# A router, attention and expert kernel: the first batch's softmax sums handed out earlier, its splits untied, one weight norm a half block later

## The chip, the core and the metric

The kernel runs on one core of a Trainium2 chip. The core has five engines with a queue of instructions each: PE (TensorE, the matrix multiplications, with its weight loads shown as PEld), DVE (VectorE), ACT (ScalarE), POOL (GpSimd) and SP (SyncE, which here issues most DMA transfers). A queue is worked off in the order in which it was written, so an instruction that waits holds up all that stands behind it on its engine. The metric is the device time of one execution in microseconds, the median of several runs.

## What is computed

The reference has three parts: an attention over 32 memory slots for 4 batches and 8 heads, a gated projection, and a mixture of experts in which each token goes to its two best of eight experts.

```python
a = np.exp(phi - np.max(phi, axis=2, keepdims=True))
a = a / (np.sum(a, axis=2, keepdims=True) + 1e-09)
k_m = np.einsum('bhsm,bhsd->bhmd', a, k)
v_m = np.einsum('bhsm,bhsd->bhmd', a, v)
scores = scale * np.matmul(q, k_m.transpose(0, 1, 3, 2))
attn = np.exp(scores - np.max(scores, axis=-1, keepdims=True))
attn = attn / (np.sum(attn, axis=-1, keepdims=True) + 1e-09)
attn_out = np.matmul(attn, v_m)
...
gate = 1.0 / (1.0 + np.exp(-(x @ w_gate)))
x = gate * (x @ w_val) @ w_out
...
noisy_logits = x @ w_gate2 + np.log1p(np.exp(x @ w_noise)) * noise
top2 = np.argpartition(-noisy_logits, 2, axis=1)[:, :2]
out[mask] += top2_w[mask, k, None] * (np.maximum(x[mask] @ w1[e], 0.0) @ w2[e])
```

There are 2304 tokens of width 512, a gated layer 1536 wide, and experts 1024 wide.

## The kernel before

Products keep nearly full precision by splitting each operand into a high and a low half of 16 bits and adding three matrix products. So every tensor that goes into a product is first split: ACT writes the high half, DVE the low one.

**The opening** does three things at once. The first is the attention of batch 0, a generator that is advanced one step at a time (`attention`): `scores` of a group makes the products on PE, then on DVE the maximum (L286) and the difference (L290) and on ACT the exponential (L291). `normalised` sums the exponentials (L297), takes the reciprocal (L300, L301) and multiplies on POOL (L302). `turned` transposes on PE (L310) and splits, the high half on ACT (L319) and the low one on DVE (L320). There are three groups; the third is the short rest of the rows. In batch 0 the sum is written into the PSUM tile of the group's own scores, so that tile is free only when L300 has read it.

The second is the preparation of the weights (`weights`, `rounded`). Each of 18 jobs (six units u of gate and value weights, 12 jobs, then six jobs of the output weights `wo`) comes in two halves of 512 KB. A half is loaded by SP (L359), its low words are scaled on ACT (L370), its high words taken apart on DVE (L374, L375), and both added on POOL (L376). The tiles that the loads land in form a ring: while the output weights are prepared it has four tiles, so the load of a half waits until POOL is done with the half four places earlier. Here the twelve halves of the output weights are called h0 to h11. ACT squares and sums each job (L399, L416). From the sums of a unit `finish` makes a power of two as its scale: `norm2` adds over the partitions on PE (L93), and DVE works out scale and inverse (L99 to L104). After the last half of `wo` all sums are joined (L421), and `wo` is split by ACT (L431) and DVE (L432).

The third is stage 1 (`stage1`, L483 on PE; L485 and L488 on ACT; L487 and L489 on DVE) of the tokens whose attention is ready. Its weights come from `fold`, which multiplies the values into a unit's weights (L257 on PE, the scale on POOL at L250, the split at L259 on ACT and L261 on DVE; for the first unit the low half is made at L1085).

**What sets the order.** `build` writes the opening out as a loop. As long as batch 0 has no tokens ready, one half of a weight is rounded (`half`), then the attention is advanced by a step. After that each call of `first` (one unit of stage 1 on 192 tokens) is followed by three steps of the weights. Between these a scheduler orders by priority, and `behind` ties an instruction after another on the same engine: here DVE's steps of the attention are tied behind the last rounding (`shifted`). Once the weights are done, SP issues 23 transfers of zeros to the output (L578) and five more (L580), then the loads for batches 2 and 3. Stage 2 (L500), the router, and the experts (L847, L861) follow.

Of the kernel before, what the change touches and what calls it, by code (L numbers as in the profile page):

```python
# [68 lines left out]
class Kern:  # L69
# [196 lines left out]
    def attention(self, b):  # L266
# [38 lines left out]
        def turned(u, ex):  # L305
            nt = 1 if u == 2 else SC
            at = ex.rearrange("p (t h) m -> p t (h m)", t=nt)
            pt = self.bank(b)
            for t in range(nt):
                self.mark = nc.tensor.transpose(pt[:, t, :], at[:, t, :], self.idf)  # L310
                if b == 1:
                    self.behind(self.mark, self.gated)
            if u == 2:
                src = pt[:, 0, :].rearrange("p (g s) -> p g s", g=2)
                oh, ol = (x[:, l, :, SC * P :] for l in range(2))
            else:
                src = pt.rearrange("p a b -> p (a b)")
                oh, ol = (x[:, l, u, : SC * P] for l in range(2))
            nc.scalar.activation(oh, src, AF.Copy, scale=2.0 ** A_BITS)  # L319
            d = nc.vector.scalar_tensor_tensor(ol, src, 2.0 ** A_BITS, oh, op0=ALU.mult, op1=ALU.subtract)  # L320
            if b < 2:
                self.behind(d, self.shifted)
        part, ex = {}, {}
        for i in range(3):
            part[i] = scores(i)
            if b == 0 and i < 2:
                yield
                continue
            for j in range(3) if b == 0 else (i - 1,) if b == 1 and i else (i,) if b > 1 else ():
                ex[j] = normalised(*part[j])  # L330
                if b == 0:
                    yield
            if b:
                yield
        if b == 1:
            ex[2] = normalised(*part[2])
        if b:
            yield
        for i in range(3):
            turned(i, ex[i])  # L340
            yield
# [36 lines left out]
    def weights(self):  # L378
# [24 lines left out]
        for n, (kind, u) in enumerate(self.wjobs):  # L403
            v = self.flat(self.W[n]) if kind != "wo" else self.flat(self.wob[u + 1]).bitcast(F32)
            for h in range(2):
                self.rounded(self.wts[2 * n + h], v[:, h * 512 : (h + 1) * 512].bitcast(I32))
                self.wload_next()
                yield
                if h == 0 and 4 <= n <= 12:
                    square(n - 1)  # L410
                if h == 0 and 2 <= n <= 12 and n % 2 == 0:
                    yield from finish(n // 2 - 1, WAIT_W)
            if kind == "wo":
                for x in [u - 1] * (u > 0) + [u] * (u == UN - 1):
# [830 lines left out]
```

## Time and profile before

| | us |
|---|---|
| median of 3 runs | 856.12 |
| the three runs | 858.1, 853.94, 856.12 |
| profiled execution, whole time | 852.53 |
| its span in the trace | 850.7 |
| outside the span | 1.83 |

PE is busy for 796.5 us of the span, 94%; DVE for 454.2, ACT for 440.6 and POOL for 232.3. The span falls into a head of some 145 us, in which all engines share the work, and a long rest in which PE is hardly ever idle. In the trace, times count from the start of the span, a matmul's row has `PE`, its weight load `PEld`, and the square brackets at a row's end give how long the engine had been idle and what ended that. The clock column is the share of TensorE's full clock that was granted: 1.00 is 2.4 GHz and 0.50 is 1.2 GHz.

### The profile page before, as it was taken

The page shows a single profiled execution, that of the slowest core. Times are in us where ns is not written, and L with a number is a line of the kernel's source. Part 1 is how long each engine was busy: PE and PEld are TensorE (multiplying, and loading weights), DVE is VectorE, ACT ScalarE, POOL GpSimd, SP SyncE. Part 2 cuts the span into 40 slices and gives each one's busy share as a digit, 9 for nine tenths or more (in the row PEclk, how much of TensorE's full clock was granted, in tenths as well). Part 3 has the DMA queues.
Part 4 walks back from the last instruction along what each step waited for, and adds up shares of the span by engine and source line. Part 5 has one row for each costly group of instructions (what it writes and reads, how often), then busy time and mean ns, then how long its engine had stood idle before and what let it go on. Part 6 is the DMA issues. An engine that isn't in the chain of part 4 may idle for free.

```text
span 850.7 us, 16713 instructions
## 1 busy us (share of the span) xinstructions
PE 796.5 (94%) x6531; PEld 521.7 (61%) x6531; DVE 454.2 (53%) x1221; ACT 440.6 (52%) x859; POOL 232.3 (27%) x257
## 2 busy tenths in 40 slices
PE   5599789999999997999999999999999999999994
PEld 3477656576677655776566555746657475574752
DVE  3988996365457776646372365643445343450210
ACT  4687786154454746534163576645557364461420
POOL 2745640112203020231135342023133231232012
PEclk9599999999999999999999999999999999999998
DMA  9987669231214654617948899535767757473112
GB/s 313 379 260 253 217 204 315 68 94 26 82 26 139 184 133 143 223 31 181 275 115 215 163 244 210 179 79 124 187 153 124 207 111 178 73 124 40 22 24 38
DMA packets 124609, 130.95 MB, mean 154 GB/s; under 512 B 71664, under 2 KB 88176, under 8 KB 124144
## 3 DMA queue, kind: packets, MB, share of 16 engines
q1 hardware_dynamic: 114480, 109.10, 44.9%
q0 software_dynamic: 10048, 20.76, 13.5%
q8 instruction: 52, 0.85, 0.4%
q14 instruction: 29, 0.24, 0.1%
HBM read 85.87 MB, written 28.76 MB: 135 GB/s over the span
## 4 chain that ended last, share of the span: by engine, by line
PE 76%; DVE 8%; DMA 6%; ACT 6%; issue 2%; POOL 1%; SPq 0%; another core or an unknown queue 0%; DVEq 0%; ACTq 0%; POOLq 0%
PE py L861 23%; PE ph L847 22%; PE px L500 14%; PE pg L483 11%; DMA st<-kv 2%; PE pv L257 2%; PE pa L282 1%; DMA wo<-wg 1%; DVE pw L374 1%; PE pa L202 1%; DMA f<-w 1%; DMA xt<-row 1%; DVE pg L487 1%; DVE gT L489 1%; DVE wq L261 1%
## 5 line engine op out<-in xcount | busy, mean ns | idle before, releaser
L483 PE MATMUL pg<-x,wq 128*128 128x192 f16 x1728 | 162.5, 249 | 14.2 <-DVE gT L489 4.8
L483 PEld LDWEIGHTS <-wq 128*128 128x128 f16 x1728 | 144.7, 99 | 33.9 <-issue 16.5
L861 PEld LDWEIGHTS <-hT 128*128 128x128 f16 (+1 forms) x960 | 99.8, 105 | 104.7 <-DVE hT L853 1.0
L500 PE MATMUL px<-wo,gT 128*128 128x512 f16 x648 | 147.9, 379 | 0.3 <-issue 0.3
L869 POOL DMA_INDIRECT out<-y,mts x40 | 64.6, 1616 | 208.5 <-ACT y L868 206.3
L861 PE MATMUL py<-w2a,hT 128*128 128x512 f16 (+1 forms) x480 | 105.3, 379 | 0.5 <-DVE hT L853 0.5
L861 PE MATMUL py<-w2b,hT 128*128 128x512 f16 (+1 forms) x480 | 104.9, 379 | 0.0
L500 PEld LDWEIGHTS <-gT 128*128 128x128 f16 x648 | 61.8, 98 | 67.9 <-issue 2.5
L853 DVE TENSOR_TENSOR hT<-r,hT 128x312 f16<-128x312 f32 (+2 forms) x128 | 57.4, 480 | 86.2 <-ACT hT L852 80.0
L847 PE MATMUL ph<-xe,w1a 128*128 128x312 f16 (+2 forms) x768 | 103.3, 296 | 0.0
L847 PE MATMUL ph<-xe,w1b 128*128 128x312 f16 (+2 forms) x768 | 103.0, 296 | 0.0
L847 PEld LDWEIGHTS <-w1b 128*128 128x128 f16 x768 | 75.2, 98 | 27.1
L847 PEld LDWEIGHTS <-w1a 128*128 128x128 f16 x768 | 75.0, 98 | 27.1
L868 ACT ACTIVATE y<-py,css 128x512 f32<-128x512 f32 (+1 forms) x40 | 27.5, 687 | 123.5 <-PE py L861 114.5
L851 ACT ACTIVATE r<-ph 128x312 f32<-128x312 f32 (+2 forms) x128 | 49.7, 429 | 76.4 <-PE ph L847 70.0
L654 POOL DMA_INDIRECT meta<-mt,vi x36 | 38.5, 1070 | 117.5 <-DVE vi L651 47.8
L832 POOL DMA_INDIRECT xg<-xs,mts x40 | 45.2, 1129 | 80.3 <-DMA xe<-xg 47.0
L485 ACT ACTIVATE sg<-pg,gss 128x384 f32<-128x384 f32 x72 | 42.0, 583 | 40.1 <-PE pg L483 37.9
L487 DVE SCALAR_TENSOR_TENSOR pg<-sg,pg 128x384 f32<-128x384 f32 x72 | 40.3, 559 | 37.5 <-PE pg L483 21.0
L488 ACT ACTIVATE gT<-pg 128x384 f16<-128x384 f32 x72 | 35.0, 486 | 36.0 <-DVE pg L487 31.0
L852 ACT CAST hT<-r 128x312 f16<-128x312 f32 (+2 forms) x128 | 53.2, 459 | 0.9
L866 DVE TENSOR_TENSOR css<-mts,iw 128x1 f32<-128x1 f32 (+1 forms) x40 | 6.4, 163 | 87.0 <-ACT y L868 80.3
(240 smaller groups left out, 943.2 us busy)
## 6 DMA issues: line engine op xcount, KB each, us to landing
wo<-w SPq DMA_DIRECT2D x52, 512.0 KB
st<-kv SPq DMA_DIRECT2D x16, 512.0 KB
w<-wo SPq DMA_DIRECT2D x12, 512.0 KB
f<-w SPq DMA_DIRECT2D x12, 512.0 KB
wsp<-hl SPq DMA_DIRECT2D x12, 512.0 KB
out<-z SPq DMA_DIRECT2D x23, 256.0 KB
xs<-row SPq DMA_DIRECT2D x18, 256.0 KB
st<-q SPq DMA_DIRECT2D x6, 576.0 KB
```

Of the source, the lines that this page charges most:

```text
L483: self.gated = nc.tensor.matmul(p[:, f, :], w[:, l, g, j, f * P : (f + 1) * P], x[:, r, g, ch * QC : (ch + 1) * QC], start=n == 0, stop=n ...
L485: self.tanh = nc.scalar.activation(sg, ps[0], AF.Tanh, scale=self.gs[(b, u)])
L487: nc.vector.scalar_tensor_tensor(pv, sg, 1.0, pv, op0=ALU.add, op1=ALU.mult)
L500: nc.tensor.matmul(p, g[:, l, f % 2, t * P : (t + 1) * P], self.wob[f // 2][:, r, f % 2, :], start=f + i == 0, stop=f == FT - 1 and i == 2)
L654: d = nc.gpsimd.indirect_dma_start(out=self.meta, out_offset=bass.IndirectOffsetOnAxis(ap=vi[:, t, k : k + 1], axis=0), in_=mt[:, t, k, :] ...
L832: self.nc.gpsimd.indirect_dma_start(out=xg.rearrange("p a b -> p (a b)"), out_offset=None, in_=self.xs[:rows, :], in_offset=bass.IndirectO ...
L847: self.first = nc.tensor.matmul(p[:, : t1 - t0], w1[:, l, k, f * P : (f + 1) * P], xe[:, x, t0:t1], start=n == 0, stop=n == 3 * KT - 1)
L851: nc.scalar.activation(r, p[:, : t1 - t0], AF.Relu, scale=2.0 ** -19)
L852: d = nc.scalar.copy(self.hT[:, 0, f, t0:t1], r)
L853: self.parted = d, nc.vector.tensor_sub(self.hT[:, 1, f, t0:t1], r, self.hT[:, 0, f, t0:t1])
L861: d = nc.tensor.matmul(py, self.hT[:, l, f, i * P : i * P + m], w2[:, w, f, :], start=n == 0, stop=n == 3 * F2T - 1)
L869: d = nc.gpsimd.indirect_dma_start(out=self.out, out_offset=bass.IndirectOffsetOnAxis(ap=mt[:m, 0:1], axis=0), in_=y[:m], in_offset=None, ...
```

## The change

Three edits, all in the opening:

- In batch 0, `attention` calls `normalised` for a group right behind the scores of the next group, as batch 1 did already, and for the third group at the end. Before, all three sums came after all three scores. The generator takes one step less before `turned`, so one half of a weight less is rounded before stage 1 begins, and from there on every rounding stands one half later beside stage 1.
- In `turned` the low half's split (L320) of batch 0 is no longer tied behind the last rounding; that of batch 1 still is.
- In `weights`, `finish` of the second unit (at job n = 4) comes after the second half of the job instead of the first.

```diff
-            if b < 2:
+            if b == 1:
                 self.behind(d, self.shifted)
         part, ex = {}, {}
         for i in range(3):
             part[i] = scores(i)
-            if b == 0 and i < 2:
-                yield
-                continue
-            for j in range(3) if b == 0 else (i - 1,) if b == 1 and i else (i,) if b > 1 else ():
+            for j in (i,) if b > 1 else (i - 1,) if i else ():
                 ex[j] = normalised(*part[j])
-                if b == 0:
-                    yield
-            if b:
-                yield
-        if b == 1:
+            yield
+        if b < 2:
             ex[2] = normalised(*part[2])
-        if b:
-            yield
+        yield
...
-                if h == 0 and 2 <= n <= 12 and n % 2 == 0:
+                if h == (n == 4) and 2 <= n <= 12 and n % 2 == 0:
                     yield from finish(n // 2 - 1, WAIT_W)
```

In the changed kernel the lines behind the first edit have numbers smaller by 7: L367, L368 there are L374, L375 here, and so on. The texts keep the numbers of the kernel before.

DVE at the second group's scores (`smx` is the maximum, `ex` the exponentials, `pa` the PSUM tile, `pmx` the sums of a norm, `wo_75` one half of a weight in its landing tile). Before:

```order
L286 TENSOR_REDUCE smx<-pa 128x16
L374 TENSOR_SCALAR pw<-wo_75 128x512
L290 TENSOR_TENSOR ex<-pa,smx 128x512
L99 TENSOR_SCALAR pmx<-pmx 128x1
L99 TENSOR_SCALAR pmx<-pmx 128x2
L102 TENSOR_SCALAR pmx<-pmx 128x1
```

And now:

```order
L286 TENSOR_REDUCE smx<-pa 128x16
L297 TENSOR_REDUCE pa<-ex 128x16
L290 TENSOR_TENSOR ex<-pa,smx 128x512
L300 TENSOR_SCALAR ssm<-pa 128x16
L99 TENSOR_SCALAR pmx<-pmx 128x1
L99 TENSOR_SCALAR pmx<-pmx 128x2
```

The first group's sum has taken the place of a rounding, which moved back.

DVE from the third group's sum on, up to stage 1. Before:

```order
L297 TENSOR_REDUCE pa<-ex 128x4
L99 TENSOR_SCALAR pmx<-pmx 128x2
L300 TENSOR_SCALAR ssm<-pa 128x4
L103 TENSOR_SCALAR sws<-pmx 128x2
L301 RECIPROCAL ssm<-ssm 128x4
L104 TENSOR_SCALAR swi<-pmx 128x2
L374 TENSOR_SCALAR pw<-wo_79 128x512
L374 TENSOR_SCALAR pw<-w_212 128x512
L375 SCALAR_TENSOR_TENSOR w_101<-wo_79,pw 128x512
L320 SCALAR_TENSOR_TENSOR x<-pa,x 128x512
```

And now:

```order
L297 TENSOR_REDUCE pa<-ex 128x4
L320 SCALAR_TENSOR_TENSOR x<-pa,x 128x512
L300 TENSOR_SCALAR ssm<-pa 128x4
L367 TENSOR_SCALAR pw<-wo_78 128x512
L301 RECIPROCAL ssm<-ssm 128x4
L367 TENSOR_SCALAR pw<-wo_79 128x512
L368 SCALAR_TENSOR_TENSOR w_101<-wo_78,pw 128x512
L320 SCALAR_TENSOR_TENSOR x<-pa,x 128x512
L320 SCALAR_TENSOR_TENSOR x<-pa,x 128x2x64
L368 SCALAR_TENSOR_TENSOR w_101<-wo_79,pw 128x512
L99 TENSOR_SCALAR pmx<-pmx 128x2
```

The splits moved ahead of two roundings, and the second unit's norm (L99) behind both.

DVE at the output weights, beside the last step of the second batch's scores; here the number of a tile tells the halves apart. Before, w64_858 is h4 and w64_867 is h5:

```order
L489 SCALAR_TENSOR_TENSOR gT_1280<-pg_1282,gT_1280 128x2x192
L301 RECIPROCAL ssm_1275<-ssm_1275 128x16
L374 TENSOR_SCALAR pw_1314<-w64_858 128x512
L374 TENSOR_SCALAR pw_1319<-w64_867 128x512
L375 SCALAR_TENSOR_TENSOR wo3_76<-w64_858,pw_1314 128x512
L375 SCALAR_TENSOR_TENSOR wo3_76<-w64_867,pw_1319 128x512
L297 TENSOR_REDUCE ssm_1323<-ex_1272 128x4
```

And now, where w64_851 is h3 and w64_858 is h4:

```order
L482 SCALAR_TENSOR_TENSOR gT_1275<-pg_1277,gT_1275 128x2x192
L301 RECIPROCAL ssm_1270<-ssm_1270 128x16
L367 TENSOR_SCALAR pw_1308<-w64_851 128x512
L367 TENSOR_SCALAR pw_1314<-w64_858 128x512
L368 SCALAR_TENSOR_TENSOR wo2_75<-w64_851,pw_1308 128x512
L368 SCALAR_TENSOR_TENSOR wo3_76<-w64_858,pw_1314 128x512
L297 TENSOR_REDUCE ssm_1318<-ex_1267 128x4
```

At the same step of the attention, each half of `wo` now stands where the one after it stood.

## Rows read from the trace of the kernel before

**Rows 1.** Page: busy time, share of the span and instructions of each engine.

```profile
PE 796.5 (94%) x6531; PEld 521.7 (61%) x6531; DVE 454.2 (53%) x1221; ACT 440.6 (52%) x859; POOL 232.3 (27%) x257
```

**Rows 2.** Busy time by stretch: from:to, length, engines, granted clock, DMA share, GB/s.

```profile
20.00:40.00 20.00, 10.76 (x82) 7.44 (x81) 17.75 (x45) 14.32 (x29) 15.95 (x18) 0.60 1.05 387
40.00:60.00 20.00, 18.87 (x236) 15.24 (x236) 17.60 (x39) 15.21 (x34) 10.23 (x11) 0.89 0.86 268
60.00:80.00 20.00, 18.92 (x244) 16.45 (x243) 17.88 (x39) 18.07 (x42) 11.78 (x15) 1.00 0.75 242
80.00:100.00 20.00, 15.73 (x198) 13.27 (x197) 17.91 (x41) 14.52 (x30) 13.22 (x17) 0.91 0.82 254
100.00:120.00 20.00, 16.14 (x208) 11.57 (x209) 17.75 (x42) 15.92 (x32) 11.09 (x30) 1.00 0.46 130
...
145.00:300.00 155.00, 151.50 (x1518) 103.12 (x1518) 92.33 (x303) 72.52 (x138) 24.34 (x39) 1.00 0.34 97
```

**Rows 3.** Chain of waits to 150 us: start, length, what was waited for.

```profile
40.44 4.20 PE pg L483 x25
...
96.72 4.80 DMA w<-wo
```

**Rows 4.** Instructions in order of time, 25 to 41 us: start, length, engine, instruction.

```profile
25.13 0.69 DVE L374 TENSOR_SCALAR pw<-wo 128x512 int32<-128x512 int32 x1
...
35.11 0.17 DVE L99 TENSOR_SCALAR pmx<-pmx 128x2 int32<-128x2 int32 x1 [1.78 <-PE pmx L93]
...
39.11 0.69 DVE L374 TENSOR_SCALAR pw<-w 128x512 int32<-128x512 int32 x1
39.70 0.68 DVE L1085 TENSOR_TENSOR wq<-pv,wq 128x512 f16<-128x512 f32 x1
...
40.44 5.78 PE L483 MATMUL pg<-x,wq 128*128 128x192 f16 x44 [0.40 <-DVE wq L1085]
```

**Rows 5.** Instructions in order of time, 89 to 113 us: the halves of wo.

```profile
90.32 1.29 POOL L376 TENSOR_TENSOR wo<-wo,w 128x512 int32<-128x512 int32 x1 [1.03 <-ACT sg L485]
...
94.16 2.54 POOL L376 TENSOR_TENSOR wo<-wo,w 128x512 int32<-128x512 int32 x2 [0.20 <-DVE wo L375]
94.21 0.67 ACT L370 ACTIVATE w<-w 128x512 int32<-128x512 uint32 x1 [0.64 <-DMA w<-wo]
...
99.71 1.29 POOL L376 TENSOR_TENSOR wo<-wo,w 128x512 int32<-128x512 int32 x1 [0.96 <-DVE wo L375]
...
101.54 0.68 ACT L370 ACTIVATE w<-w 128x512 int32<-128x512 uint32 x1 [1.05 <-DMA w<-wo]
...
105.49 0.67 ACT L370 ACTIVATE w<-w 128x512 int32<-128x512 uint32 x1 [0.55 <-DMA w<-wo]
...
109.08 2.53 POOL L376 TENSOR_TENSOR wo<-wo,w 128x512 int32<-128x512 int32 x2 [0.17 <-DVE wo L375]
```

**Rows 6.** Same view, 112 to 132 us: what follows the last half of wo.

```profile
112.92 0.16 DVE L421 TENSOR_REDUCE wom<-wom 128x1 f32<-128x6 f32 x1 [1.51 <-ACT wo L416]
112.99 0.55 DVE L487 SCALAR_TENSOR_TENSOR pg<-sg,pg 128x384 f32<-128x384 f32 x1
...
114.71 0.74 DVE L227 TENSOR_REDUCE pmx<-phi 128x1 f32<-128x576 f32 x1
...
117.70 1.28 DVE L432 SCALAR_TENSOR_TENSOR wo<-wo,wos,wo 128x1024 f16<-128x1024 f32 x1
```

**Rows 7.** As Rows 2, in two stretches of 94 to 98 us.

```profile
94.00:96.00 2.00, 0.00 (x0) 0.00 (x0) 2.00 (x7) 1.79 (x4) 1.84 (x2) 0.94 0.46 186
96.00:98.00 2.00, 1.62 (x11) 1.50 (x11) 1.32 (x4) 2.00 (x5) 1.60 (x3) 0.50 0.71 229
```

**Rows 8.** Instructions in order of time: PE behind that gap, SP's zeros and queries.

```profile
96.38 2.08 PE L483 MATMUL pg<-x,wq 128*128 128x192 f16 x12 [2.96 <-ACT sg L485]
...
113.16 17.72 SPq L578 DMA_DIRECT2D out<-z  x23
...
139.20 0.90 SPq L151 DMA_DIRECT2D st<-q  x2
```

## The prediction

> **What bounds the kernel now.** I read first how the span is shared between the engines. PE is busy for 94% of it, DVE and ACT for little over half [rows 1]. Taken as one number this says that PE sets the time and that an edit of DVE's order can't matter. So the busy time by stretch comes next [rows 2]: from 145 to 300 us PE works for 151.50 of 155.00 us, and such stretches follow to the end. A change of the opening reaches them only as a shift of their start. The opening is another matter. From 20 to 40 us PE has 10.76 us of work in 20, while DVE has 17.75, POOL 15.95, and the DMA engines are full (a share of 1.05). From 40 to 80 us PE is at 18.87 and 18.92 in 20, so it is the bound there, with DVE at 17.60 and 17.88 close behind. From 80 to 120 us PE falls to 15.73 and 16.14 and DVE stays at 17.91 and 17.75: the roundings set the pace again.
>
> The chain of waits tells where the opening is held [rows 3]: up to 40 us it runs along DVE, then along stage 1 on PE, then, at 96.72 us, through a load of a half of `wo` that takes 4.80 us to land. So there are two places to look at: the start of stage 1 near 40 us, and the output weights from 90 to 120 us. Whatever they give or take arrives at the long rest.
>
> **Edit 1 and edit 3 at the start of stage 1.** Before, DVE stands at L99 for 1.78 us, since the norm of the second unit waits for its sum on PE [rows 4]. At that place the changed order has the third group's L300, whose input has long been there; the norm's L99 now stands behind two roundings and the splits, where its input is ready. DVE also has one rounding less to do ahead of stage 1. A full-width operation of DVE costs 0.60 us, the step from one start to the next (39.11 to 39.70), though each is busy for 0.68 [rows 4]. A half takes two of these, L374 and L375: 1.2 us. This and the stall together, 3.0 us, would be the gain if DVE were the only limit, and are its upper end.
>
> It isn't. The splits that now come earlier need the transposes, these need POOL's product, and that needs the sums; the exponentials stand on ACT behind a square (L399) that waits for POOL. I laid out DVE by the new order from the operation that starts at 25.13 us [rows 4] on: ahead of the first L1085 stand 17 full-width operations, 10.2 us, about 2.2 us of small ones, and waits that I estimate at 1.4 us (0.85 for the second exponential, 0.35 and 0.2 for the first two transposed tiles). L1085 then starts at 25.1 + 13.8 = 38.9 and ends 0.68 later, at 39.6; before, it ended at 39.70 + 0.68 = 40.38, and PE went on at 40.44 [rows 4]. That is 0.8 us; since the waits are rough I take 39.8, a gain of **0.6 us**. The bounds are 0 (each wait half as long again: POOL, on which the exponentials and the splits wait, has 15.95 of 20 us of work there [rows 2]) and 2.2 us, all of the waits gone.
>
> Edit 2 has no price of its own. L320 is no longer tied behind the rounding ahead of it, so it can go in front: the move is in the order shown, and its 1.2 us lie in the sum above.
>
> Edit 3 adds a wait behind it: L99 of the second unit delays that unit's scale, and so its fold. From 40.44 us PE has stage 1 to do in a row of 44 products [rows 4], and the fold comes after it; the norm is due well before. I take it at nothing. If that cover fails, the price is at most one full-width operation, 0.6 us.
>
> **One half later, from 40 to 90 us.** From stage 1 on every rounding stands one half later, with 1.2 us of DVE work more to do behind that point. From 40 to 80 us PE is the bound and DVE has 2.40 and 2.12 us idle in 20 [rows 2], so nothing of it is seen there at first.
>
> **The output weights, from 90 to 120 us.** Here it returns. At the same step of the attention there stands now h3 where h4 stood, and h4 where h5 stood: twelve halves have to be done, and at the step where the last one was done before, one is left. The price isn't one half's 1.2 us of DVE, because the halves come in rounds: the ring of landing tiles has four places, and the load of a half waits until POOL has finished the half four before it. Before, POOL ended h3 at 90.32 + 1.29 = 91.61, h7 at 99.71 + 1.29 = 101.00 and h11 at 109.08 + 2.53 = 111.61 [rows 5]: rounds of 9.4 and 10.6 us. Now h3 stands in h4's slot. That was the first of the two products that begin at 94.16, so it ends at about 94.16 + 1.29 = 95.45, 3.84 later [rows 5]. Two rounds of 9.4 to 10.6 us after that, h11 ends between 114.25 and 116.65, so 2.6 to 5.0 us later; laid out by hand with the attention's rest, which ends earlier and frees DVE, it comes to about 115.1: **+3.5 us**.
>
> Part of this is given back. L421 before waited 1.51 us for the last squares [rows 6]. DVE's L487 (0.46 us by the steps, 0.55 busy) and L227 (0.74 us) came behind it [rows 6]; now they fit into the longer wait ahead of it. So 0.46 + 0.74 = **1.2 us** of the delay are recovered before `wo` is split at 117.70 [rows 6]. That split's delay is then 2.3 us, and what stands behind goes with it: SP's zeros, whose 23 transfers take 17.72 us from 113.16, and then the queries of batch 2 at 139.20 [rows 8], on which stage 2's companions wait just as the long rest starts. I see no reserve on this stretch of the queue, so the delay reaches the long rest.
>
> **The sum.** -0.6 + 3.5 - 1.2 = **+1.7 us**. On the profiled execution, 852.53 us with 850.7 us of span and 1.83 outside, that is 854.2. This execution is 3.6 us below the median of the three runs, 856.12; their spread, 853.94 to 858.10, is larger than the sum. I put the change on the median: **857.8 us**.
>
> **A gap that may move.** In the stretch of 94 to 96 us PE does nothing at all; its gap of 2.96 us ends with ACT's L485 [rows 7, 8], which stands on ACT behind a rounding that waited 0.64 us for its landing [rows 5]. In the next 2 us the clock is at 0.50, its lower level of 1.2 GHz, with 1.62 us of busy time [rows 7]; the same products at the full clock take half of that, so the gap costs some 0.8 to 1.0 us beyond itself. The Trainium skill, "TensorE: Matmul & The Clock Gate", section "HAM oscillation — how this bites in real kernels", says that a pause in PE's work can throw it back to half clock, so that what follows starts cold. The trace agrees: the 2.96 us gap is followed by 0.50 [rows 7]. As every half moves past this place, the gap may go or another may come; it makes one rival on each side.
>
> **The rivals.**
>
> *The ring takes up the delay.* ACT waited for landings for 0.64, 1.05 and 0.55 us in this stretch [rows 5]. If halves that come later find their loads landed, these 2.24 us are the reserve: 3.5 - 2.24 = 1.3 us remain, the 1.2 us are recovered, and the sum is -0.6 + 0.1 = -0.5, so 855.6. Against it speaks that a load starts only when POOL releases its tile, so the load moves by as much as the half four before it. For a landing the row shows 4.80 us [rows 3]. The Trainium skill, "DMA: Bandwidth & Descriptors" (section "Anatomy of one DMA — SWDGE (gpsimd) path"), fits one transfer on that path, which isn't SP's queue, by about 2.0 us and bytes over 436 GB/s: for 512 KB an estimate of 3.2 us. By it each of the two rounds could be 1.6 us shorter than now, the ring would cost 3.5 - 3.2 = 0.3, and the sum would come to about 855.6 too; the measured 4.80 us speaks against it.
>
> *Faster.* The delay is taken up as above, and ACT's L485 at 95.73 comes in time, because the rounding ahead of it no longer waits. The gap of 2.96 us and the half-clock work behind it go: -0.6 - 3.0 - 1.0 = -4.6 us, 851.5. For it speaks that stage 1's order against the roundings does change here; against it that PE isn't alone in setting the end of this stretch, the halves of `wo` are.
>
> *Slower.* ACT takes its orders in a row. When the rounding of h8 or h9 waits on ACT for a load that starts 3.8 to 5 us later, L485 and L488 of stage 1 stand behind it, PE idles, and the clock falls as in the rows above. With the ring at its upper end, 5.0, nothing recovered, and 1.0 for the clock: -0.6 + 5.0 + 1.0 = +5.4, 861.5. It decides as soon as ACT's waits for landings add up to more than the 3.5 us at which I put the ring.
>
> *The change doesn't do what it says.* The order speaks against it: the instructions do stand where the three edits put them. It would give 856.1, inside the range.
>
> **How the numbers follow.** About 0.5%, 4.3 us, is what a measurement of this kernel can tell from no change; "same" means within that, 851.8 to 860.4. The forecast of 857.8 has a chance of 0.43, the ring that takes up the delay (855.6) 0.22, faster (851.5) 0.15, slower (861.5) 0.17, no effect 0.03. Of the faster case 0.12 lies beyond 0.5%, and 0.02 comes from a start of stage 1 at its upper end; of the slower case 0.15, and 0.03 from the forecast's upper bound (1.7 + 1.5 for the ring's end, 1.2 not recovered). So faster 0.14, slower 0.18, same 0.68. The range reaches from the faster case to the slower one, 851.5 to 861.5; beyond these lie about half of the two, 0.16.
>
> **What the profile after would show.** The 1.78 us before L99 are gone, and no wait of that size stands on DVE between 30 and 40 us; the first L1085 ends at 39.4 to 40.0. If it ends at 40.4 or later, the first term is wrong. POOL ends h3 at about 95.4 and h11 at about 115.1; if h11 ends by 112.5, the ring took it up. L421 stands at about 116.4 with L487 and L227 ahead of it, the first split of `wo` (L432) at about 120.0, SP's zeros begin some 2.3 us later than 113.16. PE has a gap of about 3 us with a clock of 0.50 behind it somewhere between 94 and 100 us; without any such gap the faster case holds, with two of them the slower one. If the time moves with none of these, what is wrong is the reading that only the opening matters.

## The result

| | before, us | changed, us |
|---|---|---|
| median of 7 runs each | 855.63 | 861.40 |
| lowest to highest | 851.83 to 858.10 | 859.08 to 863.95 |
| profiled execution, whole time | 852.53 | 860.49 |
| its span | 850.7 | 858.7 |

The changed kernel is slower: its time is 1.0072 of the time before, with a 95% interval of 1.0051 to 1.0092. Timed again later, beside other runs of the kernel before, it was at 1.0062 (1.0039 to 1.0086). The forecast was 857.8, 1.7 us above the median that was known then (856.12); the measured difference is 5.8 us, and the time is nearly that of the slower rival, 861.5.

In the profile of the changed kernel, the busy time by stretch (from:to, length, busy time and instructions of PE, PEld, DVE, ACT and POOL, granted clock, DMA share, GB/s) answers to [rows 2]:

```profile
20.00:40.00 20.00, 15.27 (x89) 11.65 (x90) 15.64 (x39) 13.35 (x29) 12.40 (x13) 0.50 1.03 373
40.00:60.00 20.00, 17.75 (x179) 14.19 (x177) 16.82 (x39) 14.01 (x29) 10.94 (x13) 0.80 0.89 281
60.00:80.00 20.00, 19.24 (x257) 14.68 (x256) 16.43 (x38) 15.79 (x38) 10.87 (x16) 1.00 0.54 173
80.00:100.00 20.00, 17.11 (x222) 14.44 (x221) 16.81 (x37) 13.66 (x27) 11.15 (x14) 1.00 0.75 232
100.00:120.00 20.00, 11.14 (x118) 9.02 (x116) 16.25 (x33) 15.16 (x29) 11.16 (x11) 0.83 0.47 151
145.00:300.00 155.00, 153.17 (x1554) 105.42 (x1559) 87.42 (x286) 71.91 (x145) 23.48 (x36) 1.00 0.37 101
```

The long rest is as full as it was, 153.17 of 155 us. The loss lies ahead of it: in every stretch of 20 us from 20 to 120, DVE does 0.8 to 2.1 us less than in [rows 2], and from 100 to 120 us PE has 11.14 us of work where it had 16.14. Part of this belongs to this one execution, whose first 40 us were slow for a reason that isn't the change (last section).

The instructions of the changed kernel in order of time (start, length, engine, instruction; in the brackets the idle time before it and what ended it; line numbers smaller by 7) answer to [rows 4 to 6] and [rows 8]:

```profile
40.14 0.16 DVE L99 TENSOR_SCALAR pmx<-pmx 128x2 int32<-128x2 int32 x1
...
41.53 1.28 DVE L1078 TENSOR_TENSOR wq<-pv,wq 128x512 f16<-128x512 f32 x2
...
100.16 2.54 POOL L369 TENSOR_TENSOR wo<-wo,w 128x512 int32<-128x512 int32 x2 [0.15 <-DVE wo L368]
...
101.00 0.67 ACT L363 ACTIVATE w<-w 128x512 int32<-128x512 uint32 x1 [2.40 <-DMA w<-wo]
...
103.17 2.08 PE L476 MATMUL pg<-x,wq 128*128 128x192 f16 x12 [2.90 <-ACT sg L478]
...
119.31 2.08 PE L476 MATMUL pg<-x,wq 128*128 128x192 f16 x12 [3.46 <-ACT sg L478]
...
120.10 1.28 POOL L369 TENSOR_TENSOR wo<-wo,w 128x512 int32<-128x512 int32 x1 [1.79 <-ACT sg L478]
...
122.69 0.16 DVE L414 TENSOR_REDUCE wom<-wom 128x1 f32<-128x6 f32 x1
```

L99 stands without a wait, as was forecast. But POOL ends h3, the first of the two products at 100.16, at 101.43 where 95.45 was forecast, and h11 at 121.38 where 115.1 was. The first L1085 (now L1078) ends at about 42.2 us where 39.4 to 40.0 was forecast; a second profile of the changed kernel, below, has it at 39.2. There are two gaps of PE in place of the one of 2.96 us, 2.90 and 3.46, each behind ACT, and the granted clock is 0.50 behind both. The busy time around them, as in [rows 7]:

```profile
101.00:103.00 2.00, 0.00 (x0) 0.00 (x0) 1.81 (x5) 2.00 (x5) 2.00 (x3) 0.95 0.47 100
103.00:105.00 2.00, 1.83 (x12) 1.69 (x12) 0.37 (x2) 2.00 (x5) 0.05 (x1) 0.50 0.89 293
117.00:119.00 2.00, 0.00 (x0) 0.00 (x0) 0.88 (x3) 2.00 (x5) 1.29 (x1) 0.50 0.00 0
119.00:121.00 2.00, 1.70 (x11) 1.56 (x11) 2.00 (x4) 0.25 (x1) 0.90 (x1) 0.50 0.00 0
```

### The profile page after: what moved, and what is told of

Same layout as the page of the kernel before. It is cut to its first block, busy times and chain, and to the rows that moved or that the text cites. A ratio compares the mean times of both kernels' runs of the same rounds, so it can differ in the third digit from the quotient of the medians.

```text
span 858.7 us, 16719 instructions
## 1 busy us (share of the span) xinstructions
PE 804.5 (94%) x6531; PEld 526.6 (61%) x6531; DVE 456.1 (53%) x1221; ACT 441.3 (51%) x859; POOL 231.1 (27%) x257
## 4 chain that ended last, share of the span: by engine, by line
PE 74%; ACT 7%; DVE 5%; DMA 4%; issue 2%; POOL 0%; SPq 0%; another core or an unknown queue 0%; ACTq 0%; DVEq 0%; POOLq 0%
PE ph L840 23%; PE py L854 23%; PE px L493 14%; PE pg L476 10%; DMA w<-wo 2%; PE pv L257 1%; PE pa L282 1%; PE pa L202 1%; DMA xg<-xs,mts 1%; ACT sg L478 1%; DVE wo L425 1%; DVE wq L261 1%; ACT gT L481 1%; DVE pg L480 1%; DMA wsp<-hl 1%
## 5 line engine op out<-in xcount | busy, mean ns | idle before, releaser
L476 PE MATMUL pg<-x,wq 128*128 128x192 f16 x1728 | 165.0, 251 | 19.0 <-ACT sg L478 7.3
L476 PEld LDWEIGHTS <-wq 128*128 128x128 f16 x1728 | 146.6, 100 | 38.9 <-issue 21.4
L478 ACT ACTIVATE sg<-pg,gss 128x384 f32<-128x384 f32 x72 | 41.8, 581 | 42.1 <-PE pg L476 39.9
L480 DVE SCALAR_TENSOR_TENSOR pg<-sg,pg 128x384 f32<-128x384 f32 x72 | 40.2, 558 | 39.5 <-PE pg L476 21.0
L481 ACT ACTIVATE gT<-pg 128x384 f16<-128x384 f32 x72 | 35.0, 486 | 35.0 <-DVE pg L480 29.9
```

The lines of the kernel that those rows point to most:

```text
L476: self.gated = nc.tensor.matmul(p[:, f, :], w[:, l, g, j, f * P : (f + 1) * P], x[:, r, g, ch * QC : (ch + 1) * QC], start=n == 0, stop=n ...
L478: self.tanh = nc.scalar.activation(sg, ps[0], AF.Tanh, scale=self.gs[(b, u)])
L480: nc.vector.scalar_tensor_tensor(pv, sg, 1.0, pv, op0=ALU.add, op1=ALU.mult)
L481: nc.scalar.activation(o[:, 0, :, cols], pv, AF.Copy, scale=2.0 ** -16)
```

## Experiments: is it the later half, or the order ahead of stage 1?

The change does two things that can be had apart: the opening's instructions stand in another order, and one half of a weight less is rounded before stage 1. **e1_half_only** takes one step from the attention of the kernel before and leaves its order:

```diff
-                if b == 0:
+                if b == 0 and j != 1:
                     yield
```

> The kernel before with nothing but one step of the attention less ahead of stage 1: the sums stay behind all three scores, the splits stay tied, the second unit's norm stays where it was. From stage 1 on each rounding stands one half later, as in the changed kernel. Theory A (the later half is the cost: the output weights' last half comes one ring round later and ACT, waiting for landings, holds up stage 1): about as slow as the changed kernel, 860 to 863 us, POOL done with the last half near 118 to 121 us. Theory B (the order inside the first 40 us, and the clock that falls there, is the cost): like the kernel before, 854 to 857 us, last half near 112 to 113 us.

**e2_all_but_half** is the changed kernel with a step put back:

```diff
         if b < 2:
             ex[2] = normalised(*part[2])
+        if b == 0:
+            yield
         yield
```

> The changed kernel with one step of the attention put back ahead of the splits, so that as many halves are rounded before stage 1 as in the kernel before; all three edits of the order stay. Theory A (the later half is the cost): at the level of the kernel before or a little below, 853.5 to 856 us, last half done near 111 to 112 us. Theory B (the order inside the first 40 us is the cost): as slow as the changed kernel, 860 to 863 us, last half near 118 to 121 us.

Measured: the later half alone 1.0063 (1.0048 to 1.0078), everything but the later half 0.9982 (0.9969 to 0.9995). So the whole loss comes with the later half; theory B is out. POOL was done with the last half at 117.9 us in the first and at 111.1 us in the second.

Two runs with nothing changed gave a second profile of either kernel on the same chip, **e3_after_again** and **e4_before_again**.

> The changed kernel once more, for a second profile. In the first one the granted clock fell to 0.50 at 14 us, ten us earlier than in the profile of the kernel before. If that fall belongs to the change (theory B), it is there again, and stage 1 starts near 39.5 us; if it is an accident of one execution (theory A), the clock may stay at 1.00 to some 24 us, stage 1 starts near 37 to 39 us, and the time is 859 to 864 us all the same, with the last half of the output weights done at 117 us or later.

> The kernel before once more, for a second profile: 852 to 858 us. If the early fall of the clock is an accident of an execution (theory A), it may show here too, and then the last half of the output weights is done 1 to 3 us later than 111.6; theory B has no early fall here.

They took 852.08 and 848.47 us. In the first profile of the changed kernel the scores of batch 0 ran at half rate from 19 us on (more on that at the end); in these two, and in that of the rows ahead of the prediction, they did not. So these two are compared with each other from here on. When DVE's L487 (now L480) of some pieces of stage 1 ended, one piece being a unit on 192 tokens:

| piece | e4, before | e3, changed | difference |
|---|---|---|---|
| 1st | 45.66 | 43.44 | -2.22 |
| 4th | 54.90 | 55.13 | +0.23 |
| 11th | 84.10 | 85.09 | +0.99 |
| 14th | 95.93 | 98.16 | +2.23 |
| 18th | 114.24 | 117.87 | +3.63 |
| 21st | 128.39 | 133.09 | +4.70 |
| 35th | 221.31 | 225.80 | +4.49 |

Stage 1 does start earlier, by 2.2 us and not by 0.6 (by 1.9 against the profile of the rows ahead of the prediction, whose first piece ends at 45.29). Both parts of the change have a share: with the later half alone (e1) the first piece ends at 44.34 us, 1.0 to 1.3 earlier than in those two, and with all but the later half (e2, its last eight scores at half rate) at 44.59, 0.7 to 1.1 earlier. By these ends on DVE the gain is gone by the fourth piece; up to the eighth the two kernels are level within 0.2 us, and from the ninth on, near 75 us, the loss grows, not evenly (+3.63 at the 18th piece, +2.04 at the 19th), to the 21st. On PE the lead shrinks over a longer stretch. The first 24 products of stage 1 end 2.3 us earlier in e3, the first 48 only 1.5 us earlier: the granted clock is 0.50 up to 44.2 us in e3 and up to 44.7 in e4, so more of e3's first products ran at the lower level. The first 168 products end level, at 67 us.

The next pair takes the gain of 0.18% apart. **e16_edits_two_three** is the kernel before with the second and third edit, **e17_sums_half_kept** the first edit alone with the step put back as in e2.

> The second and third edit alone (the low splits of batch 0 untied, the second unit's norm one half later), the sums and the number of halves as in the kernel before. If these two carry the gain of the three edits with the half kept (0.998), the ratio is 0.997 to 0.999, with DVE's wait of 1.8 us at L99 gone; if the sums' place carries it, 0.999 to 1.002.

> The first edit alone with the half kept ahead of stage 1: only the place of the first two sums, one step earlier, is new. If the sums carry the gain, 0.997 to 0.999; if the other two edits do, 0.999 to 1.002.

Measured: 1.0021 (1.0006 to 1.0036) and 0.9995 (0.9975 to 1.0015). Neither carries the gain. The second and third edit without the first cost a little. The traces show why. In e16 DVE no longer waits at L99, but the untied splits now stand ahead of their inputs and wait for ACT's L319 (rows of e16):

```profile
39.31 0.69 DVE L320 SCALAR_TENSOR_TENSOR x<-pa,x 128x512 f16<-128x512 f32 x1 [1.25 <-ACT x L319]
40.92 0.69 DVE L320 SCALAR_TENSOR_TENSOR x<-pa,x 128x512 f16<-128x512 f32 x1 [0.92 <-ACT x L319]
```

With a third wait of 0.27 us e16 stands for 2.4 us at L320, more than the 1.8 us that it no longer stands at L99; its first piece ends at 49.09 us, 1.6 later than in e11, a profile of the kernel before with equally slow scores that end some 0.7 us sooner. In e3 and in e2, where the sums come earlier, the waits at L320 are 0.7 us.

## Experiments: can the half be put back later?

Theory C was that the order hands out a fixed number of roundings per piece of stage 1, so that a half which is late stays late while DVE has idle time that it can't use. The busy time by stretch in e4 (before) and then in e3 (changed), columns as above, shows that idle time:

```profile
40.00:60.00 20.00, 18.84 (x235) 14.79 (x233) 18.07 (x40) 15.33 (x35) 10.67 (x11) 0.88 0.85 268
60.00:80.00 20.00, 18.92 (x244) 16.45 (x244) 17.53 (x39) 18.10 (x42) 11.85 (x16) 1.00 0.74 239
```

```profile
40.00:60.00 20.00, 18.82 (x223) 14.23 (x220) 15.55 (x35) 14.57 (x30) 9.97 (x10) 0.89 0.82 266
60.00:80.00 20.00, 19.00 (x238) 15.76 (x237) 16.67 (x38) 16.49 (x38) 10.49 (x14) 1.00 0.63 203
```

PE's busy share is as high in the one as in the other (the next section says what it hides), but DVE does 2.5 and 0.9 us less in the changed kernel. So a half was put back there (**e5_half_back_at_u2**), and, as a control, late, where DVE has no room (**e6_half_back_at_u5**, with `(5, 0)`):

```diff
                 first(ch, u)
                 turns(weights, weights, weights)
+                if (u, ch) == (2, 2):
+                    half()
```

> The changed kernel, with one half of a weight rounded in addition behind the ninth piece of stage 1 (unit 2, third chunk, near 76 us), from where the roundings stand beside stage 1 as in the kernel before. Theory C (count: the order hands out a fixed number of roundings per piece of stage 1, so a half that is late stays late, while DVE idles in the stretch in which PE is the bound, 45 to 85 us, 8 us in all against 4.6 in the kernel before): DVE takes the half into that idle time, and the ratio to the kernel before is 0.996 to 1.001. Theory R (ring: the loads of the output weights' halves, four places, set the pace from 90 us on): much the same, 0.998 to 1.002, since the loads move with the half.

> The same half put back late, behind the sixteenth piece of stage 1 (unit 5, first chunk, near 111 us), so that the order is that of the kernel before only from there on. Theory C (count): DVE is busy for nearly all of this stretch, so the half put back delays stage 1 by its own time and little comes back: ratio 1.003 to 1.007. Theory R (ring): the half's load can't land sooner, ACT and DVE wait for it: ratio 1.005 to 1.009. A third one, T (only the last stretch counts: how many pieces of stage 1 are left when the output weights are done): all comes back, 0.997 to 1.001.

Measured: 1.0119 (1.0086 to 1.0153) and 1.0103 (1.0070 to 1.0136). Nothing came back in either; both ratios are above the changed kernel's own 1.0062 and 1.0072, though the intervals overlap. Theories C and T are out, and for e5 R as well (e6 fits R's 1.005 to 1.009 within its interval): from the place where the half is put back on, the order is that of the kernel before, and yet nothing is gained. In e5's profile the 11th piece ends at 86.60 and the 13th at 101.38 us; in e4 they are 6.14 us apart. The waits of e5 from 84 to 104 us (engine and instruction, what it waited for, us in total, times, longest):

```profile
POOL wo L369 <- DVE wo L368: 5.2, 1, 5.2
ACT w L363 <- DMA w<-wo: 3.2, 2, 2.0
...
PE pg L476 <- DVE gT L482: 2.7, 1, 2.7
PE pg L476 <- ACT sg L478: 2.4, 2, 1.6
DVE gT L482 <- ACT gT L481: 2.2, 3, 1.2
```

ACT, DVE and POOL wait here one for another in turn; ACT's wait of 2.0 us for a landing, up to 95.98 us, comes ahead of POOL's of 5.2, up to 98.34. That doesn't prove that the landings are the cause; it shows that halves which follow each other more closely aren't taken up here.

**e9_half_more_before** goes the other way: the kernel before with one more `half()` ahead of L1085.

> The kernel before with the opposite shift: one half of a weight more is rounded ahead of stage 1, so that every rounding stands one half earlier beside it. If each half that is earlier is worth what a later half costs (5.3 us at stage 1's end, less some 2 us for the later start of stage 1), the ratio is 0.995 to 0.999. If the kernel before stands where the halves come just in time (the cost has a threshold), nothing is gained and the later start shows: 1.000 to 1.006.

Measured: 1.0029 (1.0012 to 1.0045). In its profile the first piece ends at 50.91 us, 3.4 us later than in a profile of the kernel before with the same opening (e11, 47.51), and the 35th 4.6 us later. The added half stands just ahead of L1085 and so delays the start by itself, and nothing of that delay comes back up to the 35th piece. So a half earlier isn't a gain either: of the three counts tried, that of the kernel before is the fastest.

## Experiments: the norms and the ring

Which waits are new on DVE? From 45 to 76 us in e4 (before), then in e3 (changed), columns as in the last view:

```profile
DVE pg L487 <- PE pg L483: 1.3, 2, 1.1
DVE wq L261 <- ACT wq L259: 1.1, 2, 0.8
DVE gT L489 <- ACT gT L488: 0.9, 2, 0.6
```

```profile
DVE pmx L99 <- PE pmx L93: 2.3, 3, 1.2
DVE gT L482 <- ACT gT L481: 1.6, 5, 0.5
```

The largest is the norm's L99, which waits 2.3 us for PE's L93. That is the kind of wait that the change removed at 35 us; it is back at two later units' norms (0.45 us at 46.40, 1.24 at 59.09) and at that of batch 1's values (0.61 at 73.19). The second of them in e3, in order of time:

```profile
57.18 1.06 ACT L392 ACTIVATE wo<-w 128x1024 bf16<-128x1024 f32 x1
58.14 0.19 ACT L392 ACTIVATION_READ_ACCUMULATOR wo<-w 128x1 f32 x1
58.67 0.30 PEld L93 LDWEIGHTS pmx<-wum,onef 128*128 128x128 f32 x2 [0.41 <-ACT wo L392]
58.67 0.38 PE L93 MATMUL pmx<-wum,onef 128*128 128x2 f32 x2
59.09 0.17 DVE L99 TENSOR_SCALAR pmx<-pmx 128x2 int32<-128x2 int32 x1 [1.24 <-PE pmx L93]
```

ACT's square (L392, its sum read at 58.14) ends only just ahead of PE's L93, and DVE has stood for 1.24 us by then. The square comes behind the rounding that is now one half later; in e4 the L99 of the same norm, at 59.60, doesn't wait. **e8_norms_later** gives the other norms what the third edit gave the second one:

```diff
-                if h == (n == 4) and 2 <= n <= 12 and n % 2 == 0:
+                if h == (n >= 4) and 2 <= n <= 12 and n % 2 == 0:
```

> The changed kernel with the third edit widened: the norms of all units from the second to the sixth come after the second half of their job, one half later than in the changed kernel. Theory N (with the roundings one half later, DVE's L99 of the third and fourth unit reaches its place before PE has the sum: 0.5 us near 46 us and 1.9 us near 56 to 76 us in the changed kernel, none in the kernel before): these 2.4 us go, and the ratio to the kernel before falls from 1.006 to 1.002 to 1.005. Theory D (those waits lie beside work that PE sets, the loss arises from 85 us on, where ACT waits for landings): ratio stays 1.005 to 1.009.

Measured: 1.0032 (1.0014 to 1.0049), where the changed kernel had 1.0062 (1.0039 to 1.0086) on the same chip and 1.0072 at first: about half of the loss, but the intervals overlap, so the time alone doesn't settle it. The profile says where. No L99 waits from 45 to 76 us any more. At the 11th piece e8 (83.79 us) is 2.2 us ahead of e11, the kernel before with a like opening (85.96), while the first profile of the changed kernel, with that opening too, is 2.3 us behind it (88.24). e14, the changed kernel on e8's chip, comes to its 11th piece at 84.89, 1.1 us after e8, though it began 3.1 us earlier (first piece at 43.21 against 46.33). From there to the 21st piece e8 loses 6.3 us against e11.

The sizes of DVE's waits don't explain the gain up to the 11th piece: they add up to 2.3 us, the longest of them (1.24) lies where e3 and e4 stay level, and e8 is ahead of the kernel before, which has no such waits. What moves is the folds on PE. In e3 a norm's L93 stands between the products of the third unit's fold (at 45.98 us, where it waits 0.28 us for ACT's square with 14 of 32 products done); in e4 that fold runs in one piece. Busy time of PE in the 128 products of L257 for the third to the sixth unit, e4 and then e3 (from:to, length, PE, granted clock, DMA share, GB/s):

```profile
46.00:84.00 38.00, 6.33 (x128) 1.00 0.79 251
```

```profile
44.00:85.50 41.50, 8.80 (x128) 1.00 0.73 231
```

It is 6.33 us in all seven profiles that keep the half and the ring of four (before, e4, e11, and e2, e10, e16, e17 of this text), 8.80 or 8.81 in five with the later half (the first of the changed kernel, e3, e14, e1, e15), and 6.20 in e8. So the later half brings it and the place of the norms takes it away again. These 2.5 us are counted as busy time of PE: that is why PE looks as full in e3 as in e4 while its results come later.

What happens in e8 at 94 to 104 us:

```profile
96.22 2.53 POOL L369 TENSOR_TENSOR wo<-wo,w 128x512 int32<-128x512 int32 x2
...
99.55 0.68 ACT L363 ACTIVATE w<-w 128x512 int32<-128x512 uint32 x1 [4.03 <-DMA w<-wo]
...
102.23 0.56 DVE L482 SCALAR_TENSOR_TENSOR gT<-pg,gT 128x384 f16<-128x384 f32 x1 [2.04 <-ACT gT L481]
...
102.72 1.60 PE L476 MATMUL pg<-x,wq 128*128 128x192 f16 x9 [6.24 <-ACT sg L478]
```

ACT waits 4.03 us for a landing, with stage 1's own L478 and L481 queued behind the waiting rounding, and PE stands for 6.24 us. This is the mechanism of the slower rival, in e8. **e7_ring_of_five** was to remove it (with `GT = 11` for the room, and `WB` the number of landing tiles), **e15_eleven_tiles** is its control, **e14_after_timed** the changed kernel once more, and **e12_norms_ring** has both remedies:

```diff
-WB = 4
+WB = 5
-GT = 12
+GT = 11
```

> The changed kernel with five landing tiles in the ring of halves in place of four; for the room, the ring of stage 1's results has 11 tiles in place of 12. Theory R (the ring sets the pace from 90 us on, each load waiting for POOL four halves back): ACT's waits for landings go, the last half is done 2 to 4 us earlier against the pieces of stage 1, and the ratio falls to 0.999 to 1.004. Theory C (count): loads that land sooner change nothing, since the roundings stand where they stand: ratio 1.005 to 1.009.

> Both remedies together on the changed kernel: the norms of units two to six one half later (alone 1.0032) and five landing tiles (alone 1.0045; 11 tiles for stage 1's results). Theory of two causes (up to the eleventh piece of stage 1 the late half costs DVE's waits for the norms, from there on ACT's waits for landings with stage 1 behind them): the gains add, 0.998 to 1.001, and PE's wait of 6.2 us for ACT near 97 to 103 us in e8_norms_later is gone or under 3 us. One common cause, of which each remedy already took what there is: 1.003 to 1.006.

> The changed kernel itself with more rounds, beside the two above: 1.005 to 1.009 as at first, on either theory.

> The control for the ring of five: the changed kernel with 11 tiles for stage 1's results in place of 12, and the ring of four as it was. If the gain of e7_ring_of_five (1.0045 against 1.0072) is the ring's, this is at the changed kernel's level or above it, 1.005 to 1.010; if the other order that 11 tiles give is what gained, 1.003 to 1.005.

Measured: the ring of five 1.0045 (1.0024 to 1.0066), its control 1.0059 (1.0036 to 1.0082), the changed kernel 1.0062, both remedies 1.0023 (1.0007 to 1.0039). The ring's gain can't be told from its control, nor that of both from that of the norms (1.0032). In e12 the longest wait of PE for ACT is 3.3 us in place of 6.24; "gone or under 3 us" was expected, and the time hardly follows, so the clear answer of 0.998 to 1.001 did not come. Nor did a fifth landing tile take ACT's waits for landings away: 3.2 us are left in e7 and in e12. What the ring costs the changed kernel stays open.

Which waits of ACT are longer with the later half? From 88 to 126 us in e4 and then in e3:

```profile
ACT w L370 <- DMA w<-wo: 3.4, 4, 2.0
ACT wo L416 <- POOL wo L376: 2.7, 2, 1.8
```

```profile
ACT wo L409 <- POOL wo L369: 5.2, 4, 2.2
ACT w L363 <- DMA w<-wo: 3.5, 5, 1.5
```

The waits for landings hardly differ; what grows is the wait of the squares for POOL's sums. In the seven profiles named above that keep the half the squares wait 2.7 to 3.3 us, in the five with the later half 4.5 to 5.3, while the waits for landings overlap (2.2 to 4.1, and 3.0 to 4.4). PE's waits for ACT's L485 go from 4.0 to 5.7 us up to 7.0 to 8.3. No run tested the squares' waits by themselves.

The clock may have a share too. PE behind its longest gap of this stretch, e4 and then e3:

```profile
97.08 1.15 PE L483 MATMUL pg<-x,wq 128*128 128x192 f16 x12 [3.01 <-ACT sg L485]
```

```profile
115.12 2.08 PE L476 MATMUL pg<-x,wq 128*128 128x192 f16 x12 [3.33 <-ACT sg L478]
```

In e4 the clock stays at 1.00 behind a gap of 3.01 us; in [rows 8] the same gap, 2.96 us, was followed by 0.50. So such a gap can cost the clock and needn't. From 88 to 130 us the mean granted clock is 0.88 to 0.92 in the five profiles with the later half; in the seven others it is 0.96 or 1.00 but for e17, with 0.88.

Another share of the late loss is no wait at all. From the 19th to the 22nd piece, e4 (before) and then e3 (changed), busy time as above:

```profile
120.14:133.75 13.61, 12.20 (x175) 8.12 (x174) 13.41 (x28) 10.50 (x17) 1.35 (x1) 1.00 1.07 374
```

```profile
122.17:138.45 16.28, 14.43 (x214) 9.49 (x197) 15.98 (x36) 12.87 (x21) 1.23 (x2) 1.00 1.08 378
```

DVE is busy for 98% of both and has 2.57 us more to do in the second, nearly the 2.67 us by which the stretch is longer. No rounding is among it: it is one split of `wo` more (L425, 1.3 to 1.5 us), one L261 (0.7) and one L227 (0.7), work that stands behind the last half and came here with it.

**e13_half_kept_ring** is e2 with the ring of five, and **e10_half_kept_zeros_behind** is e2 with SP's zeros behind batch 2's queries, since in e2 PE waited for these queries near 144 us:

```diff
-        for i in range(NT + ST):
-            nc.sync.dma_start(self.out[i * P : (i + 1) * P, :].rearrange("p (a f) -> p a f", a=2), z2)
...
+    def zeros(self):
+        while (2, "q", 1) not in self.al:
+            yield
+        for i in range(NT + ST):
+            yield
+            d = self.nc.sync.dma_start(self.out[i * P : (i + 1) * P, :].rearrange("p (a f) -> p a f", a=2), self.z2)
+            self.behind(d, self.asked)
```

> The three edits with the half kept ahead of stage 1 (alone 0.998), and five landing tiles. If the ring bounds the kernel before too (ACT waits there 2.2 to 3.3 us for landings), the ratio is 0.993 to 0.997; if the halves come just in time there, 0.997 to 1.001.

> The three edits of the order, the half kept ahead of stage 1 as in e2_all_but_half, and SP's 23 transfers of zeros to the output put behind the loads of batch 2's queries. In e2_all_but_half PE waited for these queries near 144 us, 1.3 us, with a granted clock of 0.50 behind it, and lost 3.4 us there against the kernel before. If the zeros' transfers slowed the queries, that loss goes and the ratio falls from 0.998 to 0.993 to 0.997; if the queries are late for another reason, it stays at 0.997 to 1.000.

Measured: 0.9997 (0.9981 to 1.0013) and 0.9985 (0.9967 to 1.0003). In e10 PE's pause near 144 us is gone, but its time isn't below that of e2. Neither is better than e2, the only version here that is faster than the kernel before beyond its interval.

## Why the prediction was wrong, point by point

- **The removed stall and the start of stage 1** (-0.6 us, bounds 0 to 2.2): the direction was right and the size too small. L99 has no wait at 40.14 us, and in the pair e4 and e3 the first piece ends 2.2 us earlier. That is the upper bound. In profiles whose scores ran at half rate it was 1.0 us (46.48 against 47.51 in e11). The stall's removal isn't the gain by itself (e16 has no stall and starts later); one rounding less gives 1.0 to 1.3 us of it (e1). And I laid out the first L1085 alone: in e3 it ends 1.7 us earlier than in e4 (39.17 against 40.87), the second 2.5 us (39.77 against 42.26), since nothing stands between the two any more.
- **The second edit at nothing, the third at nothing:** neither is priced by a run alone. Together, without the first, they are 1.0021, so they aren't a gain by themselves: the untied splits wait 2.4 us for ACT (e16).
- **"From 40 to 80 us PE is the bound ..., so nothing of it is seen there at first":** this is the step that failed. In e3 the gain of 2.2 us turned into a loss of 1.0 by the 11th piece, at 85 us: 3.2 us in the stretch that the sum held at 0. By the 14th piece, at 98 us, it is a loss of 2.23, 1.2 us more, which no term had either: 4.45 us in all. A busy PE in [rows 2] was read as cover for whatever DVE does. But a half later is another order: norms came to wait for squares that were no longer ahead of them, one of them with PE's L93 inside a fold, and the folds' products took 8.80 us of PE's busy time in place of 6.33. I asked of the third edit's norm whether it has cover, and did not ask it of the four norms that the same shift moves. e8, which puts these off, has the folds at 6.20 and is 4.4 us ahead of the first profile of the changed kernel at the 11th piece, with a like opening; some 0.3% is left of that in the time.
- **The ring** (+3.5 us, bounds 2.6 to 5.0): the end of h11 moved by 4.9 us in the pair (112.31 to 117.20), inside the bounds, but not for the reason given. From h3 to h11 it took 18.90 us in e3 and 20.05 in e4, so the two rounds were not longer. What moved is h3, by 6.0 us (92.26 to 98.30) where 3.84 was forecast: it took the place of h4, as was forecast, at 98.30, but that place itself, 96.08 in e4, had moved by 2.2 us with the pieces around it. I read the place off the trace of before as if the opening ahead of it took no part.
- **The recovered 1.2 us:** wrong, 0.2 us came back. L487 and L227 did come to stand ahead of L421, which waits no more in the changed kernel. But L421 moved by 4.9 us in the pair (113.61 to 118.50), as far as h11 did, and the first split of `wo` by 4.7 (118.40 to 123.09). Between these two DVE took 4.59 us where it had taken 4.79: in the place of the work that went ahead came another piece's L487 and waits of 0.22 and 0.65 us, the longer at the norm's L99.
- **The gap's 0.8 to 1.0 us beyond itself:** true of that one execution. In e4 the same gap cost no clock.
- **"The delay reaches the long rest":** right; +4.7 at the 21st piece, +4.5 at the 35th.
- **The ring takes up the delay:** fell; nothing was taken up. Its second sum doesn't come out as written: -0.6 + 0.3 - 1.2 is -1.5, so 854.6, and 855.5 only if no more than the 0.3 is recovered. The estimate from the Trainium skill that went with it, "DMA: Bandwidth & Descriptors" (section "Anatomy of one DMA — SWDGE (gpsimd) path"), 3.2 us for 512 KB, which is made for another path than SP's queue, is not borne out on this queue: the loads of `wo` landed in 4.3 us at the median in e3, the quickest in 3.4.
- **The slower rival:** its time, 861.5, is that of the measurement, and that is in good part luck. Some of its signs are in the first profile: ACT's waits for landings between 88 and 126 us add up to 4.4 us, over the 3.5 us that I set as the point from which it decides, and there are two gaps with the clock at 0.50 behind each. But in the pair these waits are 3.5 us in the changed kernel and 3.4 in the kernel before, so they don't make the difference, and its sum held nothing for the 4.45 us before 98 us. What it had right is that PE waits longer for ACT's part of stage 1, and the lower clock with it.

What stays open: how the second part of the loss, that between the 11th and the 21st piece (3.7 us in the pair), divides between the squares' waits for POOL, the clock behind the gaps and DVE's 2.57 us; why e8 loses again there what it had gained; and why a half put back in the middle brings nothing back.

## What to carry to other kernels

When an edit takes one step out of a loop that deals out work in fixed shares, price not the edit but the shift: list every instruction whose place relative to its inputs changes, to the end of the phase, and look for the one that was just in time. A busy share of 94% on one engine did not cover the delay of another here, since 2.5 us of that busy time were the same 128 products taking longer: compare what an engine got done, not only how long it was busy. And ahead of timing such a change, separate its two effects, the new order and the shift, by giving the step back: here they were -0.18% (e2) and +0.63% (e1, in the old order).

## What was not expected of the hardware

The same 24 products of batch 0's scores took 2.98 us in some executions and 5.22 in others, of either kernel. PE, L282, in two profiles of the kernel before, e11_before_third and then e4:

> The kernel before for a third profile, on whichever chip this is. If the slow products of the scores from 18 to 28 us (218 ns each instead of 119 in four of the five profiles of kernels with the changed opening on the first chip) belong to the chip's run and not to the kernel, they may show here too, with the first piece of stage 1 done 1 us or more later than 45.3; if they belong to the changed order, they are not here.

```profile
19.34 5.22 PE L282 MATMUL pa<-kbd,gT 128*128 128x64 f32 x24
25.11 1.97 PE L282 MATMUL pa<-kbd,gT 128*128 128x64 f32 x8
```

```profile
19.27 1.90 PE L282 MATMUL pa<-kbd,gT 128*128 128x64 f32 x16
21.70 1.08 PE L282 MATMUL pa<-kbd,gT 128*128 128x64 f32 x8 [0.53 <-ACT w L370]
23.08 1.10 PE L282 MATMUL pa<-kbd,gT 128*128 128x64 f32 x8
```

That is 218 ns for a product against 119 in e4's first 16: about half the rate. Eleven of the nineteen profiles have the slow products, with the opening of either kernel and on more than one chip. So the early fall of the clock in the first profile of the changed kernel was an accident of the execution and not the change's. e11's first piece ends 1.85 us later than e4's, and its 35th still 1.7 us later. The clock column does not always tell: it was 0.50 from 14 us on in the first profile of the changed kernel, whose scores took the same 5.22 and 1.97 us, but in e11 the view of busy time shows 1.00 for them:

```profile
18.00:24.00 6.00, 5.33 (x29) 5.14 (x25) 2.98 (x5) 3.07 (x9) 2.52 (x2) 1.00 1.05 389
```

That isn't a reading of 1.00: e11's trace holds no record of the clock ahead of 46.34 us, and the view shows 1.00 where there is none. So the length of one product, not the clock column alone, has to be compared before two profiles are set side by side. What made these executions slow, no run shows.
